# One core of a local-and-pooled attention with two gated layers behind it: the first batch's four five-tap gates at other places of the written order

## The chip, the cores and the metric

The kernel runs on one core of one Trainium2 chip. The metric is the device time in microseconds (us) of one execution; of the kernel before, three runs are known: 470.57, 471.3 and 472.2 us, median 471.3.

Engines are named as in the profile: PE is TensorE (matmuls; PEld its weight loads), DVE is VectorE, ACT is ScalarE, POOL is GpSimd and SP is SyncE, which issues most of the DMAs.

## The reference

Three layers follow each other, for 4 batches of 576 positions:

```python
x = attention(q, k, v)                  # 8 heads of 64: softmax over 144 pooled positions, repeated 4 times,
                                        # plus a softmax over the positions nearer than 4
h = np.maximum(x @ w_in, 0.0)           # 512 -> 1024
conv_out[s] = sum(conv_w[k] * h[s + k - 1] for k in range(3))
x = h * sigmoid(conv_out) @ w_out       # 1024 -> 512
gate_pre[s] = sum(conv_w5[k] * x[s + k - 4] for k in range(5))
out = sigmoid(gate_pre) * (x @ w_val) @ w_out2
```

The weights arrive as 64-bit floats and are turned into 32-bit floats on the chip. Each of the large matmuls is made of three: a high part by a high part, and twice a high part by a low part.

## The kernel before, in words

The kernel is a list of named steps, `ORDER`. A loop at its end calls them in that order, and each step's instructions stand, on PE, DVE and ACT alike, behind those of the step before (`ordered`, line 144). On each engine the instructions run in the order in which they stand. So the list sets the order on every engine, and semaphores add the waits between engines.

A name is a kind and a number. The kinds that matter here:

- Attention, 16 steps of two heads each (four steps to a batch). `tpk`, `tpq`: PE transposes of k and q; `kT`, `qT` their copies by ACT; `kd`, `qd` their pooled sums on DVE. `sl` (PE): local scores into a PSUM tile of the pool `psd`, which has two tiles. `mxl`, `sub` (DVE), `xl` (ACT, the exponential), `sml`, `mul`, `tr` (DVE): the local softmax. `sd` (PE), `mxd` (DVE), `xd` (ACT, four exponentials), `smd` (DVE), `scd` (ACT), `etd` (PE), `etc` (ACT), `avd` (PE), `od` (ACT, a copy out of PSUM): the pooled softmax. `avl`, `avm` (PE): the local output in two halves, each in a `psd` tile; `xn`, `xo` (DVE) read them and so make those tiles free.
- First layer, 32 tiles of 128 rows, eight to a batch. `a` (PE, two parts of 12 matmuls to a tile), `h` (ACT, out of PSUM), then the gate: `w` (ACT, first tap), `c` (DVE, two taps), `th` (ACT, tanh), `ga` (DVE, the product), `gh` (ACT) and `gl` (DVE), its high and low part. `h` alternates between two tiles of SBUF, `h_79` and `h_80` in the built program.
- `b` (PE, four parts of 12 matmuls to a tile, four tiles to a batch) multiplies by w_out, `y` (ACT) copies the result into the batch's tile `y`.
- The five-tap gate over `y`, one for each of a batch's four tiles: `p` (ACT, the first tap, into tile `g`), `fa` and `fb` (DVE, two taps each), `ft` (ACT, tanh).
- Weights: `Ls` loads a block, `ab`, `cv`, `hi`, `lo` convert it, `Ql` adds its low part to `wout` by a DMA from POOL's queue. The staging room of some blocks is the tile `g`, that of the last block but one too, so the first `p` cannot write before that block's `Ql` has landed.

`p0` to `p3` with their `fa`, `fb`, `ft` are the first batch's gates. What they write is first read by `gv` in the last stage, at 346.8.

Of the kernel before, what the change touches and what calls it, by code (L numbers as in the profile page):

```python
# [45 lines left out]
def kernel(  # L46
# [819 lines left out]
    load(q, "ldq", 1, 0)  # L866
    ALL = ("pe", "vec", "act")
    ORDER = """
        tpk0 tpq0 kT0 kd0 qT0 sl0 qd0 sd0 mxl0 sub0 tpq1 xl0 mxd0 sml0 xd0 mul0 tpk1 tr0 qT1 smd0
        qd1 scd0 pv0 kT1 etd0 pv1 sl1 kd1 etc0 avd0 mxl1 sub1 sd1 xl1 od0 sml1 avl0 mxd1 mul1 xd1  # L870
        avm0 xn0 xo0 smd1 tpk2 xhi0 tr1 scd1 xlo0 tpq2 kT2 etd1 qT2 kd2 qd2 sl2 etc1 pv2 sd2 mxl2
        sub2 avd1 mxd2 xl2 sml2 tpk3 od1 xd2 mul2 tpq3 pv3 kT3 avl1 ab0 smd2 kd3 qT3 avm1 xn1 scd2
        qd3 sl3 xo1 ab1 cv0 xhi1 ab2 etd2 cv1 hi0 sd3 lo0 etc2 Ql0 ab3 avd2 mxl3 hi1 mxd3 cwa0
        tpq4 lo1 cwv0 xd3 Ql1 tr2 Ls5 pv4 qT4 Ls4 Lq5 sub3 od2 tpk4 smd3 xl3 Lv5 xlo1 scd3 sml3
        avl2 Lk5 kT4 mul3 etd3 xn2 cv2 avm2 etc3 a0 tr3 hi2 Ls6 xo2 ab5 cv3 avd3 xhi2 ab4 sl4 od3
        lo2 xlo2 Ls7 hi3 Ql2 cv5 sd4 lo3 avl3 Ql3 mxd4 hi5 Ls9 lo5 mxl4 sub4 xd4 Ql5 xn3 tpq5 pv5
        xl4 avm3 Lq6 smd4 qT5 sml4 scd4 Lv6 tpk5 Lw4 mul4 tr4 ab6 xo3 kT5 cv6 etd4 xhi3 sl5 etc4
        ab7 xlo3 avd4 hi6 mxl5 od4 a1 lo6 sub5 cv4 xl5 Ql6 ab9 sd5 Lk6 h0 tpq6 Ls10 mxd5 hi4 Ls8
        a2 Lq7 lo4 sml5 xd5 Ql4 mul5 a3 pv6 qT6 smd5 Lv7 cv7 cwp0 scd5 avl4 avm4 h1 a4 cwc0 Ls11
        hi7 tr5 Lw5 w1 xn4 xo4 w0 c1 etd5 lo7 a5 etc5 Ql7 c0 th1 ab10 a6 ab8 ga1 th0 cv10 tpk6 gh1  # L880
        avd5 kT6 Lk7 a7 ga0 od5 Ls13 hi10 cv8 lo10 h2 sd6 Ql10 w2 sl6 mxd6 hi8 lo8 c2 a8 xd6 Ql8
        mxl6 a9 sub6 h3 smd6 xl6 cv9 scd6 avl5 avm5 gh0 th2 sml6 a10 Lw6 hi9 xn5 lo9 xo5 ab13 tpk7
        gl0 Ql9 ab11 gl1 etd6 kT7 pv7 a11 w3 ga2 etc6 mul6 h4 tpq7 tr6 w4 c3 Ls12 avd6 gh2 Lq8 qT7
        a12 Qv8 c4 Lk8 od6 th3 sd7 gl2 th4 sl7 mxd7 ga4 xd7 a13 mxl7 sub7 gh4 smd7 avl6 ga3 xl7 h6
        avm6 sml7 h5 Lw7 mul7 gh3 a14 tr7 ab12 gl3 w5 gl4 a15 scd7 c5 w6 b0 xn6 xhi5 xo6 th5 xlo5
        tpk8 xhi4 ga5 etd7 xhi6 Lk9 xlo4 b1 h7 xlo6 kT8 c6 w7 tpq8 etc7 a16 Lq9 qT8 c7 th6 gh5
        avd7 ga6 th7 sl8 Qv9 gl5 od7 gh6 ga7 avl7 gl6 gh7 b2 mxl8 sub8 gl7 xl8 avm7 kd8 qd8 b3 Lw8
        xn7 xo7 cv11 xhi7 sd8 y0 tpk9 b4 kT9 mxd8 hi11 lo11 xlo7 b5 xd8 sml8 mul8 Lk10 a17 smd8
        tr8 Ls14 scd8 kd9 tpq9 cv12 h8 Ql11 etd8 Lq10 qT9 a18 etc8 w8 qd9 Ls15 sl9 hi12 c8 lo12
        Ql12 sd9 mxl9 th8 a19 mxd9 sub9 xd9 ga8 avd8 cv13 b6 Qv10 od8 xl9 h9 tpq10 w9 sml9 tpk10  # L890
        hi13 Lq11 qT10 b7 c9 Lk11 lo13 kT10 qd10 avl8 y1 kd10 th9 a20 xn8 ab15 ga9 ab14 cv15 a21
# [6 lines left out]
        xd11 c13 a30 h14 gl11 th13 smd11 tpk12 w14 ga13 tpq12 Lk13 kT12 c14 a31 qT12 Lq13 gh13
        kd12 th14 avl10 gl13 xhi8 avm10 ga14 xhi9 h15 xlo8 b16 Lw11 gh14 xlo9 w15 gl14 b17 scd11
        c15 b18 tr11 th15 xn10 xo10 ga15 sl12 xhi10 fb3 gh15 etd11 a32 mxl12 ft3 gl15 etc11 sub12  # L900
        b19 qd12 xl12 sml12 avd11 y4 mul12 sd12 xlo10 od11 Qv13 b20 mxd12 xd12 tpk13 b21 Lk14 kT13
        smd12 scd12 kd13 b22 tpq13 avl11 qT13 Lq14 qd13 avm11 xn11 b23 Lw12 xo11 tr12 xhi11 xlo11
        sl13 y5 a33 mxl13 sub13 xl13 etd12 h16 sml13 sd13 etc12 mul13 a34 w16 mxd13 c16 xd13 tpk14
        b24 Lk15 th16 smd13 kT14 ga16 tpq14 scd13 kd14 avd12 Lq15 b25 qT14 Qv14 od12 qd14 b26 b27
        avl12 y6 avm12 xn12 sl14 xo12 Lw13 tr13 a35 mxl14 sub14 xl14 etd13 h17 sml14 sd14 w17
        mul14 b28 etc13 mxd14 c17 xd14 tpq15 a36 th17 smd14 scd14 ga17 avd13 a37 Qv15 od13 gh16
        qT15 gl16 b29 gh17 qd15 h18 gl17 w18 b30 c18 tpk15 th18 b31 kT15 ga18 kd15 gh18 avl13 y7
        gl18 avm13 xn13 a38 tr14 Lw14 xo13 a39 a40 h19 w19 c19 a41 th19 sl15 h20 ga19 w20 etd14
        mxl15 gh19 sub15 a42 etc14 gl19 xl15 c20 avd14 a43 od14 sml15 th20 ga20 avl14 h21 mul15
        gh20 sd15 xn14 w21 gl20 avm14 mxd15 a44 Lw15 xo14 xd15 tr15 c21 a45 smd15 th21 a46 h22  # L910
        ga21 w22 a47 gh21 c22 scd15 b32 gl21 h23 xhi14 etd15 w23 xlo14 b33 etc15 c23 th22 xhi12
        avd15 ga22 xhi13 b34 xlo12 od15 gh22 xlo13 th23 gl22 avl15 ga23 avm15 xn15 gh23 a48 xo15
        gl23 xhi15 xlo15 b35 Lz0 Lz1 Lz2 a49 y8 a50 h24 w24 c24 b36 th24 b37 ga24 za0 zc0 b38 b39
        zh0 Lz3 zl0 b40 za1 y9 zc1 b41 zh1 Lz4 b42 zl1 za2 a51 zc2 b43 h25 w25 Lz5 zh2 c25 b44 y10
        zl2 th25 a52 za3 ga25 gh24 zc3 a53 gh25 za4 b45 h26 gl24 Lz6 zh3 gl25 w26 zl3 b46 za5 c26
        b47 zc5 th26 a54 y11 ga26 a55 zc4 gh26 za6 a56 h27 gl26 w27 Lz7 zc6 a57 a58 h28 c27 w28
        a59 c28 th27 ga27 a60 th28 h29 ga28 w29 a61 gh27 c29 gh28 a62 h30 gl27 th29 gl28 w30 a63
        ga29 za7 c30 gh29 b48 yh3 yh1 gl29 yh2 yl3 b49 yh0 yl1 h31 yl0 w31 b50 yl2 yh7 c31 p4 cc0
        p7 fa4 th30 yh4 th31 ga30 p6 ga31 cc1 gh30 gv0 gh31 gl30 p8 gl31 yh6 fb4 p5 b51 yh5 fa7
        ft4 b52 y12 gv1 zc7 b53 p9 b54 fa9 b55 fb9 b56 y13 fa8 ft9 b57 fb8 b58 fb7 ft8 fa6 b59 ft7  # L920
        fb6 b60 y14 fa5 ft6 b61 vh0 vl0 b62 vh1 fb5 b63 vl1 ft5 cc2 zh5 yl5 zh7 zl5 zh6 zl7 y15
        yl7 zh4 zl6 cc3 zl4 gv2 yl4 vh2 yl6 p10 vl2 cc4 yh11 gv3 yh8 fa10 yh9 vh3 fb10 yh10 p11
        cc5 vl3 ft10 yl10 yl11 fa11 d0 gv5 fb11 vh5 p13 cc6 o0 vl5 ft11 O0 yl8 gv4 fa13 p12 d1 vh4
        fb13 vl4 ft13 d2 fa12 o1 O1 fb12 d3 o2 gv6 ft12 O2 yl9 p14 vh6 fa14 cc7 o3 fb14 O3 vl6
        ft14 cc8 yh13 gv7 yh15 yl13 p15 yl15 yh12 fa15 yh14 cc9 vh7 fb15 vl7 ft15 gv8 d4 gv9 yl14
        yl12 d5 vh9 vh8 vl9 o4 vl8 O4 d6 o5 O5 d7 o6 O6 d8 o7 O7 cc10 o8 O8 cc11 gv10 vh10 vl10
        cc12 gv11 vh11 vl11 cc13 gv12 vh12 vl12 d9 gv13 vh13 vl13 cc14 o9 O9 d10 gv14 vh14 vl14
# [137 lines left out]
```

## Time and profile before

| | us |
|---|---|
| profiled execution, its own time | 469.95 |
| its span, first to last instruction | 468.2 |
| PE busy / DVE busy / ACT busy | 444.9 / 349.7 / 276.0 |
| median of the runs | 471.3 |

The profiled execution is 1.35 us under the median; 1.75 us of it lie outside the span. Busy shares over the whole span (PE 95%, DVE 75%, ACT 59%) mix stages. Times below are in us from the span's start. The first batch's gates lie between 171.8 and 215.4, in the stage where attention, the first layer and the weights' last blocks run side by side.

### The profile page before, as it was taken

What the parts mean: (1) busy time and instruction counts of PE and PEld (TensorE: products, weight loads), DVE (VectorE), ACT (ScalarE), POOL (GpSimd) and SP (SyncE); (2) the same over time, 40 slices, a digit from 0 to 9 for tenths busy, and PEclk for the clock granted to TensorE, in tenths of its full rate; (3) what the DMA queues carried; (4) which work ended last, traced back from release to release, by engine and by line L of the source; (5) the groups of instructions that cost most, each with busy time, mean ns of one, the idle gap of its engine ahead of it and who ended that gap; (6) DMA issues with size and microseconds to landing.
All of it is one profiled execution on the core that took longest, in us unless ns stands there. A gap on an engine that the chain in (4) does not pass through costs nothing.

```text
span 468.2 us, 13951 instructions
## 1 busy us (share of the span) xinstructions
PE 444.9 (95%) x5985; PEld 413.1 (88%) x5985; DVE 349.7 (75%) x613; ACT 276.0 (59%) x580; POOL 64.7 (14%) x79
## 2 busy tenths in 40 slices
...
GB/s 182 131 230 197 209 184 166 200 139 156 68 85 184 118 98 67 36 76 46 103 67 54 56 15 22 143 128 90 1 3 0 1 1 68 24 90 24 45 69 90
DMA packets 92935, 42.92 MB, mean 92 GB/s; under 512 B 69758, under 2 KB 89258, under 8 KB 92874
## 3 DMA queue, kind: packets, MB, share of 16 engines
...
q8 instruction: 47, 0.77, 0.7%
...
## 4 chain that ended last, share of the span: by engine, by line
PE 58%; DVE 27%; DMA 4%; ACT 4%; issue 3%; SPq 3%; POOL 0%; DVEq 0%; ACTq 0%
PE pa L126 13%; PE pd L126 11%; PE pb L126 10%; PE pc L126 8%; DVE cv L136 6%; PE tp L126 6%; DVE g L136 4%; PE avl L126 4%; PE sl L126 3%; DVE hglo L136 2%; DVE stage L136 2%; DVE w L136 2%; DMA ldw<-in_v_dram 2%; SPq L278 2%; PE avd L126 2%
## 5 line engine op out<-in xcount | busy, mean ns | idle before, releaser
L126 PE MATMUL pa<-xhi,win 128*128 128x288 f32 x512 | 100.3, 306 | 0.2 <-ACT h L136 0.2
L126 PE MATMUL pb<-hghi,wout 128*128 128x288 f32 x512 | 96.7, 301 | 0.0
L126 PEld LDWEIGHTS pa<-xhi,win 128*128 128x128 f32 x512 | 78.4, 193 | 2.8 <-issue 1.9
L126 PEld LDWEIGHTS pb<-hghi,wout 128*128 128x128 f32 x512 | 77.4, 191 | 1.5 <-issue 1.0
L136 DVE SCALAR_TENSOR_TENSOR cv<-h,cwt,cv 128x576 f32<-128x576 f32 x64 | 51.8, 813 | 11.3 <-ACT cv L136 10.1
L136 DVE SCALAR_TENSOR_TENSOR g<-y,cwt,g 128x576 f32<-128x576 f32 x64 | 51.7, 816 | 7.3 <-ACT g L136 5.8
L126 PE MATMUL pa<-xlo,win 128*128 128x288 f32 x256 | 55.7, 299 | 0.0
L126 PE MATMUL pb<-hglo,wout 128*128 128x288 f32 x256 | 55.4, 298 | 0.0
L126 PE MATMUL pc<-ys,wval 128*128 128x288 f32 x384 | 52.3, 294 | 0.6 <-DVE ys L136 0.6
L126 PEld LDWEIGHTS pc<-ys,wval 128*128 128x128 f32 x384 | 51.5, 188 | 1.4 <-DVE ys L136 0.8
L250 POOL DMA_DIRECT2D vd<-in_v_dram x32 | 34.3, 1073 | 111.3 <-DMA vd<-in_v_dram 58.2
L126 PE MATMUL pd<-wout,hghi 128*128 128x512 f32 x144 | 45.3, 395 | 0.0
L126 PEld LDWEIGHTS pa<-xlo,win 128*128 128x128 f32 x256 | 42.0, 192 | 0.1
L126 PEld LDWEIGHTS pb<-hglo,wout 128*128 128x128 f32 x256 | 41.8, 191 | 0.1
L126 PEld LDWEIGHTS pd<-wout,hghi 128*128 128x128 f32 x144 | 26.7, 188 | 6.0
L126 PEld LDWEIGHTS avl<-et,ldw 32*64 32x64 f32 x1536 | 26.7, 146 | 4.8 <-issue 1.8
L136 ACT ACTIVATE cv<-cv 128x576 f32<-128x576 f32 x32 | 21.8, 684 | 14.8 <-DVE cv L136 14.4
L126 PE MATMUL avl<-et,ldw 32*64 32x24 f32 x1536 | 29.2, 223 | 1.1 <-ACT ed L136 0.8
L136 ACT ACTIVATE ed<-sd,mxd 72x144 f32<-72x144 f32 x64 | 23.2, 369 | 9.0 <-DVE mxd L136 8.9
L126 PE MATMUL pd<-wout,hglo 128*128 128x512 f32 x72 | 28.5, 395 | 0.0
L136 DVE SCALAR_TENSOR_TENSOR gvf<-g,pc 128x576 f32<-128x576 f32 x16 | 11.9, 750 | 21.6 <-PE pc L126 21.6
L136 ACT ACTIVATE h<-pa 128x576 f32<-128x576 f32 x32 | 20.6, 646 | 11.5 <-PE pa L126 10.8
...
## 6 DMA issues: line engine op xcount, KB each, us to landing
...
```

Source lines behind the costliest of these rows:

```text
L126: last["pe"] = nc.tensor.matmul(*a, **kw)
L136: last[self.key] = getattr(self.engine, name)(*a, **kw)
L250: nc.gpsimd.dma_start(out=t.rearrange("p h s d -> p (h s) d"), in_=rows[:, :, r], **({"accum_op": ALU.add} if r else {}),)
L278: queue.dma_start(out=vw[KB * c : KB * c + KB, g], in_=v[0, :, k0 : k0 + KB].rearrange("h k d -> k h d"))
```

## The change

The sixteen steps `p0` to `p3`, `fa0` to `fa3`, `fb0` to `fb3`, `ft0` to `ft3` are moved in the list; no other name changes its place against another. Before, twelve of them stood in a row or nearly so behind `Ql15`; now they stand apart, with one pair of taps (`fa` or `fb`) at a time. The list is wrapped anew, so all of its lines differ; the core of it is:

```diff
-        etc9 tr9 a24 th10 Ql14 mxd10 h11 Ql15 p0 ga10 avd9 p1 fa0 b8 Qv11 od9 xd10 fa1 b9 smd10
-        sl10 fb1 scd10 tpq11 mxl10 ft1 sub10 b10 Lq12 qT11 fb0 xl10 b11 qd11 ft0 sml10 tpk11 y2
...
+        tr9 a24 th10 Ql14 mxd10 h11 Ql15 ga10 avd9 b8 Qv11 od9 xd10 b9 smd10 sl10 scd10
+        tpq11 mxl10 sub10 b10 Lq12 qT11 p0 xl10 b11 qd11 sml10 tpk11 y2 mul10 fa0 etd10
+        Lk12 a25 kT11 etc10 avl9 h12 b12 kd11 fb0 ft0 xn9 avm9 gh8 gh9 sl11 gl8 Lw10 xo9
```

On PE, POOL and SP the instructions and their order stay as they were; only DVE and ACT have another order.

On ACT, where the first `p` stood (`g<-y_2340,cwt` is `p`, `g<-g` is `ft`, `ed,smd<-sd,mxd` is `xd`, `ed<-ed,smd` is `scd`, `el<-el` is `xl`, `y_2340<-pb` is `y2`), before:

```order
L136 ACTIVATE h_80<-pa 128x576
L136 ACTIVATE g<-y_2340,cwt 128x576 x2
L136 ACTIVATE od<-avd 128x144
L136 ACTIVATE ed,smd<-sd,mxd 72x144 x4
L136 ACTIVATE ed<-ed,smd 72x144 x4
L136 ACTIVATE g<-g 128x576
L136 ACTIVATE qT<-tp 128x576
L136 ACTIVATE el<-el 128x384
L136 ACTIVATE g<-g 128x576
L136 ACTIVATE y_2340<-pb 128x576
```

The same place now:

```order
L136 ACTIVATE h_80<-pa 128x576
L136 ACTIVATE od<-avd 128x144
L136 ACTIVATE ed,smd<-sd,mxd 72x144 x4
L136 ACTIVATE ed<-ed,smd 72x144 x4
L136 ACTIVATE qT<-tp 128x576
L136 ACTIVATE g<-y_2340,cwt 128x576
L136 ACTIVATE el<-el 128x384
L136 ACTIVATE y_2340<-pb 128x576
L136 ACTIVATE kT<-tp 128x576
L136 ACTIVATE etd<-etd 72x576
L136 ACTIVATE h_79<-pa 128x576
L136 ACTIVATE g<-g 128x576
```

`od`, `xd` and `scd` stand ahead of the first `p`, which now stands just ahead of `xl`; the first `ft` stands behind `h12` and ahead of `gh8`.

On ACT about 25 us later, from `y3` on (`h_80<-pa` is `h13`, `cv<-h_80,cwt` is `w13`, `hghi<-cv` is `gh11`, `h_79<-pa` is `h14`, `cv<-cv` is `th13`), before:

```order
L136 ACTIVATE y_2340<-pb 128x576
L136 ACTIVATE g<-y_2340,cwt 128x576
L136 ACTIVATE h_80<-pa 128x576
L136 ACTIVATE cv<-h_80,cwt 128x576
L136 ACTIVATE od<-avd 128x144
L136 ACTIVATE hghi<-cv 128x576
L136 ACTIVATE ed,smd<-sd,mxd 72x144 x4
L136 ACTIVATE h_79<-pa 128x576
L136 ACTIVATE cv<-cv 128x576
```

And now:

```order
L136 ACTIVATE y_2340<-pb 128x576
L136 ACTIVATE g<-g 128x576
L136 ACTIVATE h_80<-pa 128x576
L136 ACTIVATE cv<-h_80,cwt 128x576
L136 ACTIVATE od<-avd 128x144
L136 ACTIVATE hghi<-cv 128x576
L136 ACTIVATE ed,smd<-sd,mxd 72x144 x4
L136 ACTIVATE h_79<-pa 128x576
L136 ACTIVATE g<-y_2340,cwt 128x576
L136 ACTIVATE cv<-cv 128x576
```

Ahead of `h13` stands now `ft1` in the place of `p3`, and `p2` is put between `h14` and `th13`.

On DVE at the same place (`cv<-cv,h_80` is `ga11`, `g<-y_2340,cwt,g` a pair of taps, `mxd` twice is `mxd11`, `cv<-h_80,cwt,cv` is `c13`, `smd` twice `smd11`), before:

```order
L136 SCALAR_TENSOR_TENSOR cv<-cv,h_80 128x576
L136 TENSOR_REDUCE mxd<-sd 72x4
L136 TENSOR_SCALAR mxd<-mxd 72x4
L136 SCALAR_TENSOR_TENSOR g<-y_2340,cwt,g 128x576 x2
L136 SCALAR_TENSOR_TENSOR cv<-h_80,cwt,cv 128x576 x2
L136 TENSOR_TENSOR hglo<-cv,hghi 128x576
L136 TENSOR_SCALAR smd<-smd 72x4
```

And now:

```order
L136 SCALAR_TENSOR_TENSOR cv<-cv,h_80 128x576
L136 SCALAR_TENSOR_TENSOR g<-y_2340,cwt,g 128x576 x2
L136 TENSOR_REDUCE mxd<-sd 72x4
L136 TENSOR_SCALAR mxd<-mxd 72x4
L136 SCALAR_TENSOR_TENSOR cv<-h_80,cwt,cv 128x576 x2
L136 TENSOR_TENSOR hglo<-cv,hghi 128x576
L136 TENSOR_SCALAR smd<-smd 72x4
```

The pair (`fa3` before, `fb1` now) stands ahead of `mxd11` instead of behind it. Up to `xn10` the list has seven pairs of taps before and now: before, six of them ahead of `xn9`; now, two.

## Rows read from the trace of the kernel before

**Rows 1.** Stretches: us, busy of PE, PEld, DVE, ACT, POOL, granted clock, DMA.

```profile
167.40:182.00 14.60, 11.97 (x164) 11.43 (x163) 9.09 (x18) 7.22 (x20) 4.32 (x4) 0.77 0.57 81
200.00:212.20 12.20, 12.18 (x181) 11.74 (x179) 12.02 (x21) 11.10 (x27) 3.63 (x4) 1.00 0.53 81
260.00:340.00 80.00, 79.84 (x955) 78.13 (x948) 62.76 (x103) 49.64 (x89) 1.80 (x4) 1.00 0.23 66
```

**Rows 2.** Timeline of ACT: start, duration, instruction, [idle before <-releaser].

```profile
171.81 1.44 ACT L136 ACTIVATE g<-y,cwt 128x576 f32<-128x576 f32 x2 [5.11 <-DMA wout<-stage]
173.15 0.27 ACT L136 ACTIVATE od<-avd 128x144 f32<-128x144 f32 x1
...
174.66 0.20 ACT L136 ACTIVATION_READ_ACCUMULATOR ed<-sd,mxd 72x1 f32 x1
```

**Rows 3.** Timeline of PE around its wait.

```profile
166.77 0.71 PE L126 MATMUL avd<-etd,vd 72*64 72x144 f32 x8
...
173.47 0.80 PE L126 MATMUL sl<-maskr,identr 128*128 128x256 f32 x2 [2.63 <-ACT od L136]
...
175.31 1.22 PE L126 MATMUL tp<-ident,ldq 96*128 96x96 f32 x6
176.23 0.83 PE L126 MATMUL pb<-hghi,wout 128*128 128x288 f32 x2
...
181.29 0.66 PE L126 MATMUL tp<-ident,ldk 96*128 96x96 f32 x6
```

**Rows 4.** Timeline of PE later: the same shapes, without a wait.

```profile
187.44 0.50 PE L126 MATMUL sl<-maskr,identr 128*128 128x256 f32 x2
...
188.81 0.53 PE L126 MATMUL pb<-hghi,wout 128*128 128x288 f32 x2
...
193.62 0.42 PE L126 MATMUL pb<-hghi,wout 128*128 128x288 f32 x2
...
196.88 0.71 PE L126 MATMUL avd<-etd,vd 72*64 72x144 f32 x8
```

**Rows 5.** Waits of DVE from 166.5 to 212.3: total, times, longest.

```profile
DVE g L136 <- ACT g L136: 5.6, 2, 5.2
DVE hglo L136 <- ACT hghi L136: 0.3, 1, 0.3
```

**Rows 6.** Timeline of DVE.

```profile
166.68 0.75 DVE L136 SCALAR_TENSOR_TENSOR cv<-cv,h 128x576 f32<-128x576 f32 x1
...
175.98 0.17 DVE L136 RECIPROCAL smd<-smd 72x4 f32<-72x4 f32 x1
...
177.63 0.55 DVE L136 TENSOR_REDUCE mxl<-sl 128x12 f32<-128x384 f32 x1
...
178.69 1.66 DVE L136 SCALAR_TENSOR_TENSOR g<-y,cwt,g 128x576 f32<-128x576 f32 x2
...
187.69 0.76 DVE L136 TENSOR_TENSOR hglo<-cv,hghi 128x576 fp32r<-128x576 f32 x1 [0.30 <-ACT hghi L136]
...
197.72 0.75 DVE L136 SCALAR_TENSOR_TENSOR cv<-cv,h 128x576 f32<-128x576 f32 x1
...
211.67 0.78 DVE L136 TENSOR_TENSOR xo<-avl,od 128x288 f32<-128x288 f32 x2
```

**Rows 7.** Timeline of ACT later.

```profile
198.51 0.65 ACT L136 ACTIVATE h<-pa 128x576 f32<-128x576 f32 x1
199.19 0.78 ACT L136 ACTIVATE cv<-h,cwt 128x576 f32<-128x576 f32 x1
...
202.58 0.69 ACT L136 ACTIVATE cv<-cv 128x576 f32<-128x576 f32 x1
...
214.73 0.69 ACT L136 ACTIVATE g<-g 128x576 f32<-128x576 f32 x1 [0.90 <-DVE g L136]
```

**Rows 8.** Timeline of PE at `b18` and `sl12`.

```profile
211.75 0.42 PE L126 MATMUL pb<-hghi,wout 128*128 128x288 f32 x2
212.24 0.47 PE L126 MATMUL sl<-maskr,identr 128*128 128x256 f32 x2
```

More of the change, by code (lines that the diff above doesn't have):

```diff
@@ L868 @@
     ORDER = """
[L869 to L891, printed above, removed]
@@ L892 @@
-        a22 h10 smd9 hi15 mul9 w10 cv14 avm8 scd9 a23 Lw9 lo15 xo8 hi14 c10 etd9 lo14 Ql13 sd10
-        etc9 tr9 a24 th10 Ql14 mxd10 h11 Ql15 p0 ga10 avd9 p1 fa0 b8 Qv11 od9 xd10 fa1 b9 smd10
-        sl10 fb1 scd10 tpq11 mxl10 ft1 sub10 b10 Lq12 qT11 fb0 xl10 b11 qd11 ft0 sml10 tpk11 y2
-        mul10 etd10 p2 Lk12 a25 kT11 fa2 etc10 avl9 h12 fb2 b12 kd11 ft2 xn9 avm9 gh8 gh9 sl11 gl8
-        Lw10 xo9 w12 tr10 b13 c12 a26 mxl11 gh10 sub11 th12 gl9 xl11 a27 ga12 w11 sml11 b14 mul11
-        c11 b15 gh12 gl10 th11 gl12 avd10 y3 ga11 sd11 p3 Qv12 a28 h13 mxd11 w13 fa3 od10 a29 gh11
@@ L898 @@
[L898 to L927, printed above, removed]
@@ L928 @@
-        cc15 o10 O10 d11 gv15 vh15 vl15 d12 o11 O11 d13 o12 O12 d14 o13 O13 d15 o14 O14 d16 o15
-        O15 d17 o16 O16 o17 O17
+        tpk0 tpq0 kT0 kd0 qT0 sl0 qd0 sd0 mxl0 sub0 tpq1 xl0 mxd0 sml0 xd0 mul0 tpk1 tr0
+        qT1 smd0 qd1 scd0 pv0 kT1 etd0 pv1 sl1 kd1 etc0 avd0 mxl1 sub1 sd1 xl1 od0 sml1
+        avl0 mxd1 mul1 xd1 avm0 xn0 xo0 smd1 tpk2 xhi0 tr1 scd1 xlo0 tpq2 kT2 etd1 qT2
+        kd2 qd2 sl2 etc1 pv2 sd2 mxl2 sub2 avd1 mxd2 xl2 sml2 tpk3 od1 xd2 mul2 tpq3 pv3
+        kT3 avl1 ab0 smd2 kd3 qT3 avm1 xn1 scd2 qd3 sl3 xo1 ab1 cv0 xhi1 ab2 etd2 cv1
@@ new lines @@
+        hi0 sd3 lo0 etc2 Ql0 ab3 avd2 mxl3 hi1 mxd3 cwa0 tpq4 lo1 cwv0 xd3 Ql1 tr2 Ls5
+        pv4 qT4 Ls4 Lq5 sub3 od2 tpk4 smd3 xl3 Lv5 xlo1 scd3 sml3 avl2 Lk5 kT4 mul3 etd3
+        xn2 cv2 avm2 etc3 a0 tr3 hi2 Ls6 xo2 ab5 cv3 avd3 xhi2 ab4 sl4 od3 lo2 xlo2 Ls7
+        hi3 Ql2 cv5 sd4 lo3 avl3 Ql3 mxd4 hi5 Ls9 lo5 mxl4 sub4 xd4 Ql5 xn3 tpq5 pv5 xl4
+        avm3 Lq6 smd4 qT5 sml4 scd4 Lv6 tpk5 Lw4 mul4 tr4 ab6 xo3 kT5 cv6 etd4 xhi3 sl5
+        etc4 ab7 xlo3 avd4 hi6 mxl5 od4 a1 lo6 sub5 cv4 xl5 Ql6 ab9 sd5 Lk6 h0 tpq6 Ls10
@@ new lines @@
+        mxd5 hi4 Ls8 a2 Lq7 lo4 sml5 xd5 Ql4 mul5 a3 pv6 qT6 smd5 Lv7 cv7 cwp0 scd5 avl4
+        avm4 h1 a4 cwc0 Ls11 hi7 tr5 Lw5 w1 xn4 xo4 w0 c1 etd5 lo7 a5 etc5 Ql7 c0 th1
+        ab10 a6 ab8 ga1 th0 cv10 tpk6 gh1 avd5 kT6 Lk7 a7 ga0 od5 Ls13 hi10 cv8 lo10 h2
+        sd6 Ql10 w2 sl6 mxd6 hi8 lo8 c2 a8 xd6 Ql8 mxl6 a9 sub6 h3 smd6 xl6 cv9 scd6
+        avl5 avm5 gh0 th2 sml6 a10 Lw6 hi9 xn5 lo9 xo5 ab13 tpk7 gl0 Ql9 ab11 gl1 etd6
+        kT7 pv7 a11 w3 ga2 etc6 mul6 h4 tpq7 tr6 w4 c3 Ls12 avd6 gh2 Lq8 qT7 a12 Qv8 c4
@@ new lines @@
+        Lk8 od6 th3 sd7 gl2 th4 sl7 mxd7 ga4 xd7 a13 mxl7 sub7 gh4 smd7 avl6 ga3 xl7 h6
+        avm6 sml7 h5 Lw7 mul7 gh3 a14 tr7 ab12 gl3 w5 gl4 a15 scd7 c5 w6 b0 xn6 xhi5 xo6
+        th5 xlo5 tpk8 xhi4 ga5 etd7 xhi6 Lk9 xlo4 b1 h7 xlo6 kT8 c6 w7 tpq8 etc7 a16 Lq9
+        qT8 c7 th6 gh5 avd7 ga6 th7 sl8 Qv9 gl5 od7 gh6 ga7 avl7 gl6 gh7 b2 mxl8 sub8
+        gl7 xl8 avm7 kd8 qd8 b3 Lw8 xn7 xo7 cv11 xhi7 sd8 y0 tpk9 b4 kT9 mxd8 hi11 lo11
+        xlo7 b5 xd8 sml8 mul8 Lk10 a17 smd8 tr8 Ls14 scd8 kd9 tpq9 cv12 h8 Ql11 etd8
@@ new lines @@
+        Lq10 qT9 a18 etc8 w8 qd9 Ls15 sl9 hi12 c8 lo12 Ql12 sd9 mxl9 th8 a19 mxd9 sub9
+        xd9 ga8 avd8 cv13 b6 Qv10 od8 xl9 h9 tpq10 w9 sml9 tpk10 hi13 Lq11 qT10 b7 c9
+        Lk11 lo13 kT10 qd10 avl8 y1 kd10 th9 a20 xn8 ab15 ga9 ab14 cv15 a21 a22 h10 smd9
+        hi15 mul9 w10 cv14 avm8 scd9 a23 Lw9 lo15 xo8 hi14 c10 etd9 lo14 Ql13 sd10 etc9
+        tr9 a24 th10 Ql14 mxd10 h11 Ql15 ga10 avd9 b8 Qv11 od9 xd10 b9 smd10 sl10 scd10
+        tpq11 mxl10 sub10 b10 Lq12 qT11 p0 xl10 b11 qd11 sml10 tpk11 y2 mul10 fa0 etd10
@@ new lines @@
+        Lk12 a25 kT11 etc10 avl9 h12 b12 kd11 fb0 ft0 xn9 avm9 gh8 gh9 sl11 gl8 Lw10 xo9
+        w12 tr10 b13 c12 a26 p1 mxl11 gh10 sub11 th12 gl9 xl11 a27 ga12 w11 fa1 sml11
+        b14 mul11 c11 b15 gh12 gl10 th11 gl12 avd10 y3 ga11 fb1 ft1 sd11 Qv12 a28 h13
+        mxd11 w13 od10 a29 gh11 xd11 c13 a30 h14 p2 gl11 th13 smd11 tpk12 w14 ga13 fa2
+        tpq12 Lk13 kT12 c14 a31 qT12 Lq13 gh13 kd12 th14 avl10 gl13 fb2 ft2 xhi8 avm10
+        ga14 xhi9 h15 xlo8 b16 Lw11 gh14 xlo9 w15 gl14 p3 b17 scd11 c15 b18 tr11 fa3
@@ new lines @@
+        th15 xn10 xo10 ga15 sl12 xhi10 fb3 gh15 etd11 a32 mxl12 ft3 gl15 etc11 sub12 b19
+        qd12 xl12 sml12 avd11 y4 mul12 sd12 xlo10 od11 Qv13 b20 mxd12 xd12 tpk13 b21
+        Lk14 kT13 smd12 scd12 kd13 b22 tpq13 avl11 qT13 Lq14 qd13 avm11 xn11 b23 Lw12
+        xo11 tr12 xhi11 xlo11 sl13 y5 a33 mxl13 sub13 xl13 etd12 h16 sml13 sd13 etc12
+        mul13 a34 w16 mxd13 c16 xd13 tpk14 b24 Lk15 th16 smd13 kT14 ga16 tpq14 scd13
+        kd14 avd12 Lq15 b25 qT14 Qv14 od12 qd14 b26 b27 avl12 y6 avm12 xn12 sl14 xo12
```

27 lines of the change are left out of this document (added).

## The prediction, made before the changed kernel ran

> **What bounds the kernel now.** I read the stretches first, then the timelines of ACT, PE and DVE around the first batch's gates, then the waits of DVE. PE is the engine that sets the end: in the 80 us from 260 on it is busy for 79.84 [rows 1], so whatever PE is late or early at 260 goes through to the end. The question is thus what the change does to PE before that.
>
> The only long wait of PE in this part is the one in [rows 3]: 2.63 us until `od10`. The reason stands on ACT [rows 2]: `p0` waits 5.11 us for the landing of a low part of w_out, with `od10` behind it. That wait costs PE a second time. From 167.4 to 182 the mean granted clock is 0.77 [rows 1]; `sl10` takes 173.47 to 175.31, 1.84 us, where a later `sl` takes 187.44 to 188.81, 1.37; the 24 matmuls of `b10` and `b11` take 176.23 to 181.29, 5.06 us, where 24 others take 193.62 to 196.88, 3.26 [rows 3, 4]. That is the lower of the two clock levels (1.2 instead of 2.4 GHz), and it costs 0.47 + 1.80 = 2.27 us (`tpq11` not counted).
>
> DVE must be looked at too. From 200 to 212.2 it is busy for 12.02 of 12.20 us, PE for 12.18 [rows 1]: both are full. What ties them is `sl12`: it needs a `psd` tile that `xn10` makes free. `xn10` starts at 211.67 and, as one of two in 0.78, ends near 212.06 [rows 6]; `b18` is through at 211.75 + 0.42 = 212.17; `sl12` starts at 212.24 [rows 8]. So DVE and PE arrive there together. There is no slack for DVE.
>
> **The change part by part.**
>
> *On PE.* Nothing is added or moved. `p0` no longer stands ahead of `od10`, so `sl10` can start when `b9` is through, at 173.47 - 2.63 = 170.84. PE's gain at this place is 2.63 + 2.27 = 4.9 us. `p0` now comes to its turn behind `qT11`, after 172.2, and the landing was at 171.8 [rows 2], so it finds its data; none of the moved steps issues a DMA, and POOL's and SP's queues are as they were.
>
> *On DVE.* The moved taps cost the same: a pair 1.66 us [rows 6]. Up to `xn10` the same instructions stand on DVE before and now, seven pairs of taps among them. So `xn10` moves by the difference of DVE's idle time ahead of it, and by nothing else. Before, that idle time is 5.6 + 0.3 = 5.9 us [rows 5]: DVE lay idle while `p0` waited, and then had twelve taps to run without any wait. Now:
>
> 1. DVE is free at 166.68 + 0.75 = 167.43 [rows 6]. Its next work but `smd10` is `mxl10`, which needs `sl10`: 170.84 + 1.37 = 172.21. Idle 4.78, less `smd10`, two instructions of 0.17 [rows 6]: 4.44 us. (`smd10` itself is ready in time: `avd10` ends at 166.77 + 0.71 = 167.48 [rows 3], and from `od10` to the last exponential ACT takes 174.86 - 173.15 = 1.71 [rows 2].) The old wait is thus still there for DVE, nearly whole; only the taps that filled DVE behind it are gone from that place.
> 2. `p0` stands on ACT just ahead of `xl10`, half of 1.44 us [rows 2]; `sml10` waits for `xl10`, and DVE has `qd11` beside it. 0 to 0.72, I take 0.4.
> 3. `ft0` stands ahead of `gh8` on ACT and waits for the second tap of `fb0`. `gl8` waits for `gh8`. After `fb0` ACT needs twice 0.69 (a copy or tanh of this shape, [rows 7]), DVE has `xn9`, half of 0.78: idle 1.0 (0 to 1.4).
> 4. From `gl8` to `ga11` DVE ran without a wait before, and nothing new stands in its way. Then `fb1`, and behind its second tap `ft1` (0.69), `h13` (199.19 - 198.51 = 0.68) and `w13` (0.78) on ACT [rows 7] before DVE's `c13` can start: 2.15 us, in which DVE has only `mxd11`, a reduction over as many values as a `ga`, some 0.75. Idle 1.4 (0 to 2.15). Before, `p3`, which waits for nothing late, stood where `ft1` stands now.
> 5. `th13` follows `w13` by 202.58 - 199.19 = 3.39 us on ACT [rows 7]; `p2` now adds 0.72, and `th13` takes 0.69: 4.8. DVE has from `c13`, 0.78 after `w13`'s start, 1.66 for it, 0.76 for `gl11`, 0.34 for `smd11`: 3.54. `ga13` waits 1.3 (0 to 1.9).
> 6. `ft2` stands ahead of `xhi8` as `ft0` ahead of `gh8`: 2 x 0.69, less `ga14`'s 0.75: 0.6 (0 to 1.4).
> 7. `gl14`, whose `gh14` now stands behind all of these on ACT: 0 to 0.7, I take 0.3.
>
> The sum is 4.44 + 0.4 + 1.0 + 1.4 + 1.3 + 0.6 + 0.3 = 9.4 us, 3.5 more than 5.9 (bounds: 4.4 to 12.7, that is 1.5 less to 6.8 more). `xn10` and with it `sl12` are 3.5 us later, at 215.7.
>
> *PE at `sl12`.* Its work up to `b18` ends 4.9 us earlier than 212.17, or up to some 2 us later than that where it waits for `h13`. So it waits 6 to 8 us at `sl12`, in place of the 2.63 us at `sl10`. After the old wait the clock was low for a while and 2.27 us were lost; `etd`, `a` and `b` behind `sl12` are the same kind of work, and I charge the same, 2.3 (0 if the clock stays; 2.7 if all shapes lose). Before, PE was there at 212.24 with the old loss already in it, so both add up: 3.5 + 2.3 = 5.8 us later.
>
> *Behind `sl12`.* DVE has no more of the moved taps but `fb3`, which stood there before too. PE is the bound from here on [rows 1], so the 5.8 us stay.
>
> The profiled execution took 469.95 us (468.2 of span and 1.75 around it): 469.95 + 5.8 = 475.75. It lies 1.35 us under the median of the runs, 471.3, so I expect a median of 471.3 + 5.8 = 477.1.
>
> **The rivals.**
>
> A. *PE keeps what it gains.* If nothing holds `sl12`, the 4.9 us go through: 466.4 us. For it: the wait that goes is PE's longest in the stage, and PE is the bound later. Against it: [rows 6, 8], no slack at `sl12`. Between PE and DVE the stretch from 200 to 212.2 does not decide by busy shares, 12.18 against 12.02 of 12.20 [rows 1]. The Trainium skill (Perfetto Trace Analysis, Identifying the Most-Contended Engine) says that matmul busy time is no good measure for TensorE, that its weight-load share is one, and that for VectorE the busy share is fair. By that rule the weight loads' 11.74 us in [rows 1] stand below DVE's 12.02, DVE is the contended engine of this stretch, and an earlier PE is worth nothing there; going by matmul share one would forecast 466.4. The trace agrees with the rule in that `sl12` starts 0.2 us behind `xn10`'s end.
>
> B. *ACT's order costs DVE nothing.* If items 3 to 7 come to nothing, DVE idles 4.8 us instead of 5.9 and `sl12` comes 1.1 us earlier. PE still waits there for some 4 us and may lose 0 to 2.7 us to the clock: 470.2 to 472.9. For it: before, ACT was idle often enough to be waited for by DVE only 0.3 us in this stretch outside the taps [rows 5]. Against it: an `ft` waits for its taps by its nature, as `ft3` does before (0.90, [rows 7]), and what stands behind it must wait too.
>
> C. *It costs more.* If PE's waits for `h13` and `h14`, which now come late, also lower the clock ahead of `sl12`, another 2.3 us may go: 479.4.
>
> That the change would not do what it says (`p0` still waiting, now ahead of `xl10`) needs a landing 1.4 us later than in [rows 2]; I give it no chance of its own, and it would only add to the forecast.
>
> **How the numbers follow.** Forecast 0.68, between 474.5 and 479; C 0.10; B 0.14; A 0.08. A measurement of this kernel tells 0.3% from no change, 1.4 us: faster is under 469.9, slower over 472.7. B falls on three sides: with 0.05 below 469.9 (less idle time still, and no loss of clock), 0.05 within, 0.04 above. So faster is 0.08 + 0.05 = 0.13, same 0.05, slower 0.68 + 0.10 + 0.04 = 0.82. The range 471.5 to 480.0 leaves out A and the lower half of B.
>
> **What would show it.** In the profile of the changed kernel ACT's first `g<-y,cwt` has no wait for `wout<-stage`, and PE no wait for `od` near 170.8: the first step. DVE's waits up to `xn10` sum to more than 5.9 us, with `cv` and `hglo` waiting for ACT, and ACT's `g<-g` waiting for DVE in three places: items 3 to 6. PE waits 4 us or more for DVE at one `sl` near 209 to 216, and the clock is low behind it. If that `sl` waits under 2 us, or DVE's waits sum to less than 5, I am wrong; if both hold and the time is still near 471, the lateness was made good somewhere behind 220, against [rows 1].

## The result, and the profile after

The changed kernel takes 479.0 us, the median of 14 runs (473.08 to 481.19), beside 472.03 for the kernel before, also of 14. The ratio is 1.0123 with a 95% interval of 1.0081 to 1.0164: 0.0123 x 472 = 5.8 us slower (3.8 to 7.7). The ratio is one of means and leaves out disturbed runs, one of 601.45 us before and three over 480.2 after, and so is not the quotient of the medians. The forecast was 5.8 us, to a median of 477.1, slower with a chance of 0.82.

The profiled execution took 479.7 us, its span is 477.9. That is 9.7 more than before, and not all of it is the change. The clock line of the page (40 slices, tenths of full speed) of after, and below it that of before:

```profile
PEclk9755555999999999997999999999999999999999
```

```profile
PEclk9775575999999998999999999999999999999999
```

In the first seven slices, up to 84 us, the clock was low for longer in after. When `b8` starts, ahead of the first moved step, after is already 4.28 us late (171.69 against 167.41). The four experiments made from the changed kernel's list run the same list up to there and start `b8` at 166.43 to 170.62; so this part differs from one execution to the next. It goes with the clock: over the first 90 us the mean granted clock is 0.64 in after and in the two runs that start `b8` at 169.47 and 170.62, and 0.68 to 0.72 in the four that start it at 166.43 to 167.41. Which of the two brings the other is not shown. From here on I count from the start of `b8`. The rows of `b8` and `b20` before, and of `b8`, `sl10` and `sl11` after ([rows 3, 4, 8] have the others of before):

```profile
167.41 0.53 PE L126 MATMUL pb<-hghi,wout 128*128 128x288 f32 x2
...
218.70 0.54 PE L126 MATMUL pb<-hghi,wout 128*128 128x288 f32 x2
```

```profile
171.69 0.53 PE L126 MATMUL pb<-hghi,wout 128*128 128x288 f32 x2
...
174.97 0.40 PE L126 MATMUL sl<-maskr,identr 128*128 128x256 f32 x2
...
186.25 0.50 PE L126 MATMUL sl<-maskr,identr 128*128 128x256 f32 x2
```

In us from `b8`, each step at the start of its first row on PE, "end" the last instruction of the kernel:

| kernel | `sl10` | `sl11` | `sl12` | `b20` | end | `sl12` to `b20` |
|---|---|---|---|---|---|---|
| before | 6.07 | 20.04 | 44.83 | 51.29 | 300.76 | 6.46 |
| after | 3.28 | 14.57 | 48.73 | 56.98 | 306.23 | 8.25 |
| after less before | -2.79 | -5.47 | +3.90 | +5.69 | +5.47 | +1.79 |

PE gains 5.47 us by `sl11`, is 3.90 us late at `sl12`, 5.69 at `b20`, and then little changes: 249.25 us from `b20` to the end, 249.47 before. The later slice that differs in the clock lines (the 8 at 176 to 187 us in before, the 7 at 215 to 227 in after) shows the same thing: PE's wait went from one place to another.

The waits of PE between 182 and 221 in after (engine and tile, what was waited for: total, times, longest):

```profile
PE sl L126 <- DVE xo L136: 7.1, 1, 7.1
PE avl L126 <- ACT kT L136: 0.6, 1, 0.6
PE tp L126 <- ACT ed L136: 0.6, 1, 0.6
PE pa L126 <- ACT y L136: 0.2, 1, 0.2
```

The wait of [rows 3] for `od` is gone, and one of 7.1 us for DVE's `xo`, which is `xn10`, has come. PE at that place in after (start, duration, instruction, idle before and releaser), which answers to [rows 8]:

```profile
212.89 0.43 PE L126 MATMUL pb<-hghi,wout 128*128 128x288 f32 x2
220.41 0.77 PE L126 MATMUL sl<-maskr,identr 128*128 128x256 f32 x2 [7.09 <-DVE xo L136]
...
222.22 1.17 PE L126 MATMUL etd<-ident,ed 72*72 72x72 f32 x8
```

`b18` is through at 213.32, `sl12` starts at 220.41. Its first matmuls take 0.77 us instead of 0.47 in [rows 8], so the clock is low. The stretches of after say the same (us, busy of PE, PEld, DVE, ACT, POOL, granted clock, DMA):

```profile
171.69:220.42 48.73, 39.90 (x655) 37.57 (x653) 38.53 (x64) 29.99 (x65) 8.86 (x10) 0.98 0.42 68
220.42:228.67 8.25, 8.25 (x147) 7.40 (x147) 6.80 (x13) 4.04 (x7) 0.27 (x1) 0.72 0.01 2
218.29:225.12 6.83, 4.71 (x114) 4.44 (x115) 6.76 (x13) 3.42 (x6) 0.00 (x0) 0.50 0.01 2
```

The clock stands at 0.50, 1.2 GHz, from 218.29, while PE still waits, to 225.12. From `sl12` to `b20` PE is busy for the whole 8.25 us, and only slower: this is the 1.79 us of the table.

What DVE waited for between 171.69 and 218.5 in after, which answers to [rows 5]:

```profile
DVE cv L136 <- ACT cv L136: 2.6, 2, 1.3
DVE mxl L136 <- PE sl L126: 2.4, 1, 2.4
DVE smd L136 <- ACT ed L136: 2.3, 1, 2.3
DVE hglo L136 <- ACT hghi L136: 1.2, 2, 1.0
DVE xlo L136 <- ACT xhi L136: 0.7, 1, 0.7
DVE sml L136 <- ACT el L136: 0.3, 1, 0.3
DVE qT L136 <- ACT qT L136: 0.3, 1, 0.3
```

With the timeline's two digits this is 9.72 us. Before it was 5.92 (5.9 in [rows 5]), so 3.80 us more, and `sl12` is 3.90 later. Four of the waits, on DVE's timeline:

```profile
173.56 0.17 DVE L136 TENSOR_SCALAR smd<-smd 72x4 f32<-72x4 f32 x1 [2.27 <-ACT ed L136]
...
185.63 0.76 DVE L136 TENSOR_TENSOR hglo<-cv,hghi 128x576 fp32r<-128x576 f32 x1 [0.96 <-ACT hghi L136]
...
201.72 1.67 DVE L136 SCALAR_TENSOR_TENSOR cv<-h,cwt,cv 128x576 f32<-128x576 f32 x2 [1.24 <-ACT cv L136]
...
205.68 0.76 DVE L136 SCALAR_TENSOR_TENSOR cv<-cv,h 128x576 f32<-128x576 f32 x1 [1.33 <-ACT cv L136]
```

These are `smd10`, `gl8`, `c13` and `ga13`. Why `c13` waits stands on ACT's timeline, just ahead of it:

```profile
199.64 0.69 ACT L136 ACTIVATE g<-g 128x576 f32<-128x576 f32 x1 [2.37 <-DVE g L136]
200.24 0.63 ACT L136 ACTIVATE h<-pa 128x576 f32<-128x576 f32 x1
200.90 0.78 ACT L136 ACTIVATE cv<-h,cwt 128x576 f32<-128x576 f32 x1
```

ACT stands still for 2.37 us at `ft1`, which waits for the taps `fb1` on DVE; `h13` and `w13` stand behind it, and DVE's next piece of work, `c13`, waits for `w13`.

### The profile page after: what moved, and what is told of

The parts are those of the page before. It is cut to its first block, busy times and chain, and to the rows that moved or that the text cites. A ratio compares the mean times of both kernels' runs of the same rounds, so it can differ in the third digit from the quotient of the medians.

```text
span 477.9 us, 13950 instructions
## 1 busy us (share of the span) xinstructions
PE 448.4 (94%) x5985; PEld 415.4 (87%) x5985; DVE 350.5 (73%) x613; ACT 275.4 (58%) x580; POOL 65.1 (14%) x79
## 4 chain that ended last, share of the span: by engine, by line
PE 62%; DVE 21%; DMA 5%; ACT 5%; SPq 3%; issue 2%; DVEq 0%; ACTq 0%
PE pa L126 14%; PE pd L126 11%; PE pb L126 10%; PE pc L126 8%; PE tp L126 6%; DVE g L136 6%; DVE cv L136 6%; PE avl L126 5%; PE sl L126 3%; DVE hglo L136 2%; DMA ldw<-in_v_dram 2%; DMA ldq<-in_q_dram 2%; DVE w L136 2%; PE avd L126 2%; PE etd L126 2%
## 5 line engine op out<-in xcount | busy, mean ns | idle before, releaser
L126 PE MATMUL pb<-hghi,wout 128*128 128x288 f32 x512 | 95.5, 298 | 0.0
L126 PEld LDWEIGHTS pb<-hghi,wout 128*128 128x128 f32 x512 | 76.2, 188 | 1.6 <-issue 1.0
L126 PEld LDWEIGHTS avl<-et,ldw 32*64 32x64 f32 x1536 | 27.7, 152 | 5.8 <-issue 2.5
L126 PE MATMUL avl<-et,ldw 32*64 32x24 f32 x1536 | 30.2, 227 | 1.9 <-ACT ed L136 1.0
L136 DVE SCALAR_TENSOR_TENSOR cv<-cv,h 128x576 f32<-128x576 f32 x32 | 23.9, 750 | 4.8 <-ACT cv L136 4.8
```

The lines of the kernel that those rows point to most:

```text
L126: last["pe"] = nc.tensor.matmul(*a, **kw)
L136: last[self.key] = getattr(self.engine, name)(*a, **kw)
```

## The experiments

Four of them only move names in the list, one adds matmuls. A line of a diff is a piece of the list. Times of steps are from the start of `b8`; a table of all stands at the end of this section.

**The four tanhs behind the stage.** From the changed kernel's list; only `ft0` to `ft3` move. Three of them stood ahead of `sl12`; `ft3` stood behind it already.

```diff
-        b12 kd11 fb0 ft0 xn9
+        b12 kd11 fb0 xn9
...
-        ga11 fb1 ft1 sd11
+        ga11 fb1 sd11
...
-        gl13 fb2 ft2 xhi8
+        gl13 fb2 xhi8
...
-        mxl12 ft3 gl15
+        mxl12 gl15
...
+        y5 ft0 a33
+        y6 ft1 avm12
+        avl13 ft2 y7 ft3 gl18
```

> The changed kernel with only its four tanhs (ft0 to ft3) moved on ACT, each to a place some 30 us or more later where its taps have long been done; all taps stay. Times are counted from the start of b8 (the first matmul of the third w_out tile). Changed kernel: sl12 starts 48.7 us after b8 and waits 7.1 us. Theory T (DVE's idle time ahead of xn10 sets sl12, and most of the new idle time is ACT standing in an ft): the waits of DVE behind a tanh go (1.0 + 1.2 + 1.3 + 0.7 + 0.3 us of 9.7, about 3 to 4 us net), sl12 at 45.0 to 46.0, its wait still about 6 us, b20 at about 54, time 3 us under the changed kernel. Rival L (the taps, put into a stretch where DVE is full, are the whole cost; the tanhs do not matter): sl12 at 48.7 as in the changed kernel, time the same.

Measured: 476.19 us, ratio 1.0075 (1.0043 to 1.0106) to the kernel before. `sl12` stands at 45.94 and `b20` at 54.06, as the theory said. What DVE waits for ACT in the gates is now this:

```profile
DVE cv L136 <- ACT cv L136: 0.9, 1, 0.9
DVE hglo L136 <- ACT hghi L136: 0.8, 1, 0.8
```

So 48.73 - 45.94 = 2.79 us of the 3.90 at `sl12` were the tanhs on ACT that wait for their taps, with other work behind them. PE still waits 6.0 us for `xo`, and from `sl12` to `b20` it takes 8.12 us, the clock's price again (the granted clock is 0.50 from 214.13 to 220.95):

```profile
216.56 0.76 PE L126 MATMUL sl<-maskr,identr 128*128 128x256 f32 x2 [6.01 <-DVE xo L136]
```

At the end of the trace 306.23 - 303.87 = 2.36 us of the gain are left, a little less than the 3 us expected. The ratios say 2.3 us, but their intervals overlap, so the executions' times alone do not show it.

**Only the blocking step moved.** From the kernel before: the first taps go behind `xd10`, so that `od9` and the exponentials of `xd10` are ahead of the wait, and the other taps stay.

```diff
-        h11 Ql15 p0 ga10 avd9 p1 fa0 b8 Qv11 od9 xd10 fa1 b9
+        h11 Ql15 ga10 avd9 b8 Qv11 od9 xd10 p0 p1 fa0 fa1 b9
```

> The kernel before with one part of the change alone: p0, p1 and fa0 stand behind xd10 instead of ahead of od9, so od9 no longer waits behind p0; the other taps stay in a row. Counted from b8; kernel before: sl10 at 6.1, sl12 at 44.8, b20 at 51.3. Rival P (PE's stall at sl10 is worth its 2.63 us and the clock behind it, 4.9 us): sl12 at about 40, time about 466. Theory T (DVE's idle time is the same, since the taps still start when the landing comes, and sl10's scores are read only behind the taps): sl10 at 3.2, but PE waits some 3 us a little later, at tpk11, for DVE; sl12 at 44.5 to 45.2, b20 at 51 to 51.8, time within 1 us of the kernel before.

Measured: 471.98 us, ratio 1.0012 (0.9968 to 1.0057): no difference. `sl10` stands at 3.28, as early as in after, but `sl12` at 44.43 and `b20` at 50.90, within 0.4 of before (and 0.1 under what was expected). The waits of PE from 160 to 262 show where the 2.79 us went:

```profile
PE tp L126 <- issue: 3.1, 1, 3.1
PE pa L126 <- issue: 0.4, 1, 0.4
PE sl L126 <- DVE xo L136: 0.2, 1, 0.2
```

The transposes of `tpk11` start at 181.07 after 3.13 us of idle time (the view names no releaser):

```profile
181.07 0.93 PE L126 MATMUL tp<-ident,ldk 96*128 96x96 f32 x6 [3.13 <-issue]
```

On DVE the `sub10` of that moment, behind the taps and behind DVE's wait of 5.68 us for the first of them, ends at 180.98:

```profile
174.81 3.26 DVE L136 SCALAR_TENSOR_TENSOR g<-y,cwt,g 128x576 f32<-128x576 f32 x4 [5.68 <-ACT g L136]
...
180.42 0.56 DVE L136 TENSOR_TENSOR el<-sl,mxl 128x384 f32<-128x384 f32 x1
```

0.09 us later PE goes on. The kernel says why it must wait for `sub10`: `sl` and the transposes take the two `psd` tiles in turn, only `tpq11` takes one between `sl10` and `tpk11`, and so `tpk11` gets the tile of `sl10`, which `sub10` is the last to read. So taking the wait away at `sl10` alone is worth nothing, since DVE is no earlier.

**Three pairs behind `sl12`.** From the changed kernel's list; `fa2`, `fb2`, `fa3` no longer stand ahead of `xn10`.

```diff
-        w14 ga13 fa2 tpq12
+        w14 ga13 tpq12
...
-        gl13 fb2 ft2 xhi8
+        gl13 xhi8
...
-        tr11 fa3 th15 xn10 xo10 ga15 sl12 xhi10 fb3 gh15 etd11 a32 mxl12 ft3 gl15 etc11 sub12 b19
+        tr11 th15 xn10 xo10 ga15 sl12 xhi10 gh15 etd11 a32 mxl12 gl15 fa2 etc11 sub12 fb2 b19
...
+        xlo10 ft2 fa3 od11
+        mxd12 fb3 xd12
+        avm11 ft3 xn11
```

> The changed kernel with three pairs of taps (fa2, fb2, fa3) and their tanhs moved behind xo10 (and fb3 a little later). Counted from b8. Theory T: xn10 comes earlier by 3 x 1.6 us of taps and by the wait behind ft2 (0.7 to 1.0), sl12 at 42.5 to 43.5 with a wait of 1 to 1.5 us in place of 7.1, so no low clock behind it; b20 at 50.5 to 51.5, about 5.5 to 6.5 us under the changed kernel. Rival (sl12 waits for something else than the taps ahead of xn10): sl12 stays at 48.7.

Measured: 472.36 us, ratio 1.0021 (0.9984 to 1.0058): no difference to before, and 0.0102 x 472 = 4.8 us better than after. PE in this run:

```profile
210.06 0.47 PE L126 MATMUL sl<-maskr,identr 128*128 128x256 f32 x2 [1.27 <-DVE xo L136]
```

The wait is 1.27 us, `sl12` stands at 42.94 (5.79 us earlier than in after), the first row takes 0.47 us, and the clock is 1.00 all the way to `b20`. Three pairs are 3 x 1.66 [rows 6] = 4.98 us of DVE, and the wait behind `ft2` (0.65 for `xlo8`) goes with them: 5.63. So DVE's work and waits ahead of `xn10` set `sl12`. From `sl12` to `b20` it is 7.67 us instead of 6.46, by a wait for DVE's `qd12`, which now stands behind two of the pairs:

```profile
217.09 0.71 PE L126 MATMUL sd<-kT,qT 64*72 64x144 f32 x8 [1.15 <-DVE qT L136]
...
210.06:217.73 7.67, 6.52 (x146) 5.72 (x146) 6.96 (x12) 4.02 (x7) 0.74 (x1) 1.00 0.06 13
```

At `b20` the gain over after is 6.37 us; behind it 1.52 are given back, 1.0 of them in a wait for ACT's `qT`. So at the end it is 4.8 us and not the 5.5 to 6.5 that were expected.

**PE kept busy in the wait.** From the changed kernel; 36 matmuls that nothing reads stand behind `b18`.

```diff
+    def filler(i):
+        E["pa", 2 * KF] = p = mpair("pa")
+        for n in range(36):
+            u = n % 2
+            mm(
+                p[:, u, :SH],
+                wout[0][:, 0, :128],
+                hg(0)[0][:, 0, u * SH : u * SH + SH],
+                start=True,
+                stop=True,
+            )
...
-        c15 b18 tr11
+        c15 b18 dm9 tr11
...
+        F["dm9"] = lambda: filler(9)
```

> The changed kernel with 36 more matmuls on PE between b18 and sl12, whose results are not used (they go into the PSUM tile that a32 overwrites). They can start when h15 has made that tile free and run for 36 x 0.133 = 4.8 us inside PE's wait of 7.1 us. DVE and ACT are unchanged. Counted from b8; changed kernel: sl12 at 48.7, b20 at 57.0, 8.25 us from sl12 to b20 where the kernel before takes 6.46. Theory T (that difference of 1.8 us is the granted clock, which fell while PE stood idle): sl12 still at 48.6 to 48.9, but 6.4 to 6.6 us to b20, no stretch of low clock near 220, b20 at 55.2, time 1.8 us under the changed kernel. Rival (the stages behind sl12 are longer for another reason, as a late DVE or ACT): 8.25 us to b20 as before.

Measured: 475.78 us, ratio 1.0117 (1.0078 to 1.0155). The place itself went as the theory said: `sl12` at 48.72 as in after, with a wait of only 0.41 us left, and from there to `b20` 6.47 us instead of 8.25. The stretch from `sl12` to `b20` in this run:

```profile
215.43:221.90 6.47, 6.47 (x147) 5.72 (x147) 6.33 (x13) 4.04 (x7) 0.26 (x1) 1.00 0.01 3
```

The same 147 matmuls, at a clock of 1.00 instead of 0.72: the 1.8 us are the clock's. But the whole was not seen to come 1.8 us earlier: the ratio is that of after, though its interval of 3.6 us in width could hide such a gain. In the trace `b20` is 1.79 us earlier than in after and the end 0.88 later. The place of the loss is 27 us behind `b20`, inside `sl14`:

```profile
247.39 0.77 PE L126 MATMUL sl<-kT,qT 64*24 64x32 f32 x69
249.09 0.33 PE L126 MATMUL sl<-kT,qT 64*24 64x32 f32 x27 [0.92 <-issue]
```

PE pauses for 0.92 us between two matmuls of one group, and the clock is low from 249.74 to 253.15; from `sl14` to `sl15` this run takes 26.38 us, after 23.78, that is 2.60 more. What makes the pause stays open: the view gives no releaser, and one trace does not tell whether it comes in every execution. So the clock's part is shown at its place, and what it is worth at the end of the kernel is not.

**Five pairs behind `sl12`.** If DVE's queue ahead of `xn10` is what counts, the gain at `sl10` can be kept. From the changed kernel's list (all tanhs go later too, and `p0` steps behind `xl10`):

```diff
-        qT11 p0 xl10 b11
+        qT11 xl10 p0 b11
...
-        fb0 ft0 xn9
+        fb0 xn9
...
-        a26 p1 mxl11
+        a26 mxl11
...
-        w11 fa1 sml11
+        w11 sml11
...
-        th11 gl12 avd10 y3 ga11 fb1 ft1 sd11 Qv12 a28 h13 mxd11
+        th11 p1 gl12 avd10 y3 ga11 sd11 Qv12 a28 h13 p3 mxd11
...
+        mul12 fa1 sd12 xlo10 ft0 od11
+        b22 fb1 tpq13
+        sub13 ft1 xl13
+        xd13 fa2 tpk14 b24 fb2 Lk15
+        b26 fa3 b27
+        sub14 ft2 xl14
+        avd13 fb3 a37
+        y7 ft3 gl18
```

(`p2` now stands behind `Lk13`; `fa2`, `fb2`, `fa3` and the old places of `p2`, `p3` are taken out.)

> A version after theory T: p0, fa0 and fb0 where the changed kernel has them, every other tap behind sl12 in the stretch where DVE lay idle (fa1 behind mul12, fb1 behind b22, the rest up to avd13), each tanh tens of steps behind its taps. Only the list is changed. Theory T: PE waits neither at sl10 nor at sl12 (under 0.3 us); sl12 at 39 to 39.5 from b8, b20 at 45.3 to 46, where the kernel before has 44.8 and 51.3; nothing is given back behind it; time 5.5 to 6 us under the kernel before, near 466. Rival L2 (the taps cost the same wherever they stand, since DVE or ACT is late behind 220 as well): the gain up to b20 is lost by 260, time near the kernel before.

Measured: 467.77 us, ratio 0.9892 (0.9849 to 0.9935), faster than the kernel before and than after: 5.1 us under before by the ratio, 5.65 in the trace, where 5.5 to 6 were expected. PE around `sl12`, and the stretch from there:

```profile
205.26 0.42 PE L126 MATMUL pb<-hghi,wout 128*128 128x288 f32 x2
205.55 0.47 PE L126 MATMUL sl<-maskr,identr 128*128 128x256 f32 x2
```

```profile
205.50:212.00 6.50, 6.50 (x148) 5.75 (x146) 5.78 (x12) 3.68 (x7) 0.40 (x3) 1.00 0.29 44
```

PE waits nowhere for more than 0.2 us from 160 to 300, and the clock is not low between 81 and 460. DVE waits longer than before ahead of `xn10`, 7.5 us in sum instead of 5.9. From 164.5 to 205.2 the longest are these:

```profile
DVE mxl L136 <- PE sl L126: 2.4, 1, 2.4
DVE smd L136 <- ACT ed L136: 1.7, 1, 1.7
DVE hglo L136 <- ACT hghi L136: 1.2, 1, 1.2
DVE cv L136 <- ACT cv L136: 1.1, 2, 0.7
```

That costs nothing, because ahead of `xn10` DVE has five pairs, 5 x 1.66 [rows 6] = 8.3 us, less to do, and only the first gate's two pairs left.

All seven from `b8` on:

| kernel | `sl10` | `sl12` | `b20` | end | wait at `sl12` | ratio to before |
|---|---|---|---|---|---|---|
| before | 6.07 | 44.83 | 51.29 | 300.76 | none | 1 |
| after | 3.28 | 48.73 | 56.98 | 306.23 | 7.1 | 1.0123 |
| four tanhs late | 3.28 | 45.94 | 54.06 | 303.87 | 6.0 | 1.0075 |
| first taps only | 3.28 | 44.43 | 50.90 | 300.91 | 0.2 | 1.0012 |
| three pairs late | 3.28 | 42.94 | 50.61 | 301.38 | 1.3 | 1.0021 |
| PE kept busy | 3.28 | 48.72 | 55.19 | 307.11 | 0.4 | 1.0117 |
| five pairs late | 3.28 | 39.12 | 45.58 | 295.11 | none | 0.9892 |

The end counted from `b8` (one trace of each kernel) and the ratio (many executions) give the same difference to before within 0.9 us in all six (after: 5.47 and 5.8). So the 4.28 us by which the profiled execution of after was late at `b8` are not part of what the change costs.

## Why the prediction was right, step by step

The mechanism was right, and the sum (5.8) met the measured ratio (5.8), with 5.69 in the trace at `b20`. That they meet to a tenth is luck: the interval reaches from 3.8 to 7.7 us, and errors cancelled inside the sum, as follows.

- *PE at `sl10`.* Forecast a gain of 2.63 + 2.27 = 4.9; measured 2.79 at `sl10` and 5.47 at `sl11`, the rest being the clock over all of the stretch and not only over the shapes that I compared.
- *DVE ahead of `xn10`.* The prediction's seven items, forecast and measured:

| item | place | forecast | measured |
|---|---|---|---|
| 1 | `smd10`, `mxl10` | 4.44 | 2.27 + 2.41 = 4.68 |
| 2 | `sml10` (behind `p0`), and `qd11` | 0.4 | 0.32 + 0.29 = 0.61 |
| 3 | `gl8` (behind `ft0`) | 1.0 | 0.96 |
| 4 | `c13` (behind `ft1`) | 1.4 | 1.24 |
| 5 | `ga13` (behind `p2`) | 1.3 | 1.33 |
| 6 | `xlo8` (behind `ft2`) | 0.6 | 0.65 |
| 7 | `gl14` | 0.3 | 0.25 |
| | sum | 9.4 | 9.72 |

  Less 5.9 this is 3.8 instead of 3.5, and `sl12` came 3.90 late. Item 1 had one step wrong: that `smd10` would find its data. It waited 2.27 us for ACT's exponentials, where the prediction put the whole wait at `mxl10`. As both wait within the same stretch, the sum hardly changed. In item 2 the 0.29 us of `qd11` are a wait for `qT11`, which stands ahead of `p0`; only the 0.32 are `p0`'s.

  The premise that `xn10` moves by DVE's idle time "and by nothing else" does not hold quite. `ga10` and `xn10` in after:

```profile
170.54 0.75 DVE L136 SCALAR_TENSOR_TENSOR cv<-cv,h 128x576 f32<-128x576 f32 x1
...
219.82 0.81 DVE L136 TENSOR_TENSOR xo<-avl,od 128x288 f32<-128x288 f32 x2
```

  From one to the other it is 49.28 us, before 44.99 [rows 6]: 4.29 more, of which idle time explains 3.80. The other 0.49 fit the six waits that after has more (nine for three): a row of DVE that waits for nothing often starts some 0.08 us before the row ahead of it ends, one that waits does not, and 6 x 0.08 = 0.48; that is an estimate. `sl12` still came only 3.90 late because DVE stood 0.42 us earlier against `b8` here (`ga10` starts 1.15 us ahead of it, before 0.73). So the close match of 3.80 and 3.90 is in part luck too.
- *PE at `sl12`.* Forecast a wait of 6 to 8 us; measured 7.09.
- *The clock behind it.* Forecast 2.3, taken over from the old place; measured 1.79. It is the term of the last sum (3.5 + 2.3) that was most off, and the run with PE kept busy shows that it is the clock's. The errors of the two, +0.4 and -0.5, cancelled.
- *Behind `sl12`.* As good as nothing made good: 249.25 us from `b20` on against 249.47. Of the sixteen steps named in the change `fb3` and `ft3`, which stand here, kept their places.

The names `od10` and `avd10` in the prediction are `od9` and `avd9` in the list; the rows meant are the same.

Of the rivals, A (PE keeps 4.9 us) falls: the 5.47 us were there at `sl11` and gone at `sl12`. The run with the first taps alone says it too, and the last one shows the condition under which A would have held: DVE early at `xn10`. On the rule of the Trainium skill (Perfetto Trace Analysis, Identifying the Most-Contended Engine), the trace agrees that DVE, not PE, decided at that place. In after, from 200 to 220, DVE again has the larger share, 16.24 us against 10.97 of the weight loads:

```profile
200.00:220.00 20.00, 11.90 (x174) 10.97 (x173) 16.24 (x26) 14.67 (x33) 3.64 (x4) 0.96 0.36 61
```

But neither is full, and the share does not say what `sl12` waits for: DVE's work and its idle time ahead of `xn10`, taken together. B (ACT's order costs nothing) falls with items 3 to 7: together 4.43 us, and 2.79 us come back when the tanhs leave. C (the clock falls twice) falls: from 182 to 218.2 the granted clock is 1.00, and PE has no wait for `h13` or `h14` in its list.

The signs that the prediction named held. ACT's first `p` had no wait for the landing:

```profile
177.65 0.77 ACT L136 ACTIVATE g<-y,cwt 128x576 f32<-128x576 f32 x1
```

And its `g<-g` waited for DVE in three places ahead of `sl12`, for 0.75 us, 2.37 (shown above) and 2.23:

```profile
184.34 0.69 ACT L136 ACTIVATE g<-g 128x576 f32<-128x576 f32 x1 [0.75 <-DVE g L136]
...
212.55 0.69 ACT L136 ACTIVATE g<-g 128x576 f32<-128x576 f32 x1 [2.23 <-DVE g L136]
```
